# Longformer attention and a cosine-gated MLP on one core: the front's DMA order behind waits for value blocks, six MLP units moved into the front

## The chip, the core and the metric

The kernel runs on one of the eight cores of a Trainium2 chip. The metric is device time in microseconds (us) of one execution. The profile is of one execution, taken by the hardware profiler; its times are counted from the start of its span. Five engines work beside each other, each through its own list in order: TensorE (PE, matmuls; PEld is its weight load), VectorE (DVE), ScalarE (ACT), GpSimd (POOL), and SyncE (SP), which here only issues DMAs. POOL issues DMAs too, all those that change the type of the data on the way. DMAs of both run on the same 16 DMA engines.

## What is computed

The reference, cut to its core: attention over 8 batches of 8 heads with 576 positions of 64, in which a position sees its neighbours up to 32 away and 8 global positions, which also see all; then an MLP on the 4,608 rows of 512.

```python
mask = np.abs(pos[:, None] - pos[None, :]) <= 32
mask = mask | is_global[:, None] | is_global[None, :]
scores = np.where(mask, scale * np.matmul(q, k.transpose(0, 1, 3, 2)), -1e9)
attn = softmax(scores)                     # by rows
x = np.matmul(attn, v).transpose(0, 2, 1, 3).reshape(4608, 512)
h = x @ w_in                               # 512 x 2048
out = (h * np.cos(h)) @ w_out              # 2048 x 512
```

## The kernel before

**Units of work.** Attention goes by pairs of heads (32 pairs, four to a batch), two pairs to a step s (s=0 to 15). Inputs come in half batches, which are the two pairs of one s. The MLP goes by 9 tiles of 512 rows; one *unit* ("1", `one`, `mlp_in`) is one of 16 column blocks of a tile: four matmuls into ph, the cosine (L500, ScalarE), the product g (L501, VectorE). An *out* ("2", `two`, `mlp_out`) is four matmuls of the second layer; every fourth is followed by a copy of po and a store.

**Order.** It is written out by hand: each engine's list is the order in which the program's lines call it. A string of steps is walked through, FRONT for the first four pairs, THIRD for s=2, ORDER for s=3 on. Letters with a pair's number: k and q (`local_k`, `local_q`: transposes on PE and evictions into kw and qb, L406 to L437), s (`scores`: matmuls, exponential L449, mask L450), p (`values`: matmuls into pv, the one PSUM tile for it, then the division into xn, L463 to L469), x (`turn_x`: transposes into xT; after a batch's fourth pair POOL copies the 8 global columns, L489), g (`globals_kq`: POOL copies global keys and queries into kw and qb), n (`x_squares`, ScalarE).

**DMAs.** POOL issues, in one queue: L (`load_qk`, k and q of a half batch with a cast, L257), c (`cast_half`, v of a half batch to fp16 in DRAM, L246), W (`load_w_in`, a quarter of w_in, L642), O (`load_w_out`, a quarter of w_out, L646), gathers of the global rows (L284), casts of k and q to DRAM (L250, half batch 4 on). SP issues, in one queue: the value blocks of a pair from the cast v into vw (`load_v`, L296 to L304; four buffers), the global values from vgw (`load_vg`, L309), transposing loads of k and q (L262, L263), stores. A pair's value block is 2,688 rows of 128 bytes: (80 + 32) x 2 and 2 x 11 x 112.

**Steps that matter below.** In s=2 "G" (`casts`) makes POOL wait, by copying one element of xn into gate (L672), and then gather k, q and v of the next global rows; "b" (`copy_globals`) makes ScalarE copy the gathered kg and qg (L368), "t" turns them. "I" loads eight indices into POOL's registers (L662). A unit may be called only for a tile whose rows are ready (`ready`). In the front, `turned` takes its PSUM from the tag "h", later from "s".

```python
        STEPS = {"s": scores, "p": values, "x": turn_x}
        ...
        for s in range(2, B * NP // 2):
            outs_by[0] = 4 * (s - 2) if s < 5 else 8 * (s - 3)
```

Of the kernel before, what the change touches and what calls it, by code (L numbers as in the profile page):

```python
# [9 lines left out]
FP32 = mybir.dt.float32  # L10
FP16 = mybir.dt.float16
# [6 lines left out]
B, H, S, D = 8, 8, 576, 64  # L18
NT, DM, DFF = 4608, 512, 2048
P = 128  # L20
# [3 lines left out]
G = 8  # L24
# [14 lines left out]

ORDER = "sa0 sa1 sa2 2 2 2 sz0 2 sz1 sz2 pa 1 1 2 xa pz G 1 1 2 xz n 1 1 2 kc qc 1 b kd qd 2 t 1"  # L40

THIRD = "sa0 sa1 sa2 sz0 sz1 sz2 1 1 pa 1 1 xa pz G 1 1 kc qc xz 1 1 b kd qd 1 n t 1"

FRONT = ("g0 s0.0 s0.1 s0.2 c1 k1 q1 g1 B s1.0 s1.1 s1.2 v2 v3 g2 g3 W0 L2 c2 k2 q2 p0 s2.0 x0 s2.1 s2.2 W1 I "
         "k3 q3 p1 s3.0 x1 s3.1 s3.2 L3 c3 g4 g5 k4 q4 p2 v4 v5 W2 x2 p3 W3 k5 q5 x3 n0 v6 v7 g6 g7 O0 O1 O2 O3")
OK_ALL = float(P * (B * NP * 2 * BP + B))


def view(ap, *dims):

    return bass.AP(ap.tensor, ap.offset, [ap.ap[0], *[list(d) for d in dims]])


def dview(ap, offset, *dims):

    return bass.AP(ap.tensor, ap.offset + offset, [list(d) for d in dims])
# [134 lines left out]
def kernel(  # L191
# [10 lines left out]
    nc = tc.nc  # L202
# [5 lines left out]
    keep = es.enter_context(tc.tile_pool(name="keep", bufs=1))  # L208
    work = es.enter_context(tc.tile_pool(name="work", bufs=2))
    ps = es.enter_context(tc.tile_pool(name="ps", bufs=2, space=PSUM))  # L210
# [4 lines left out]
    zero16 = const.tile([P, 1], FP16)  # L215
# [15 lines left out]
    NV = 4  # L231
# [4 lines left out]
    vw = [keep.tile([P, 2, NB, D + 1], FP16, name=f"vw{i}") for i in range(NV)]  # L236
# [4 lines left out]
    def cast_half(s, which):  # L241

        base = s * 4 * S * D
        for x in which:
            if x == "v":
                nc.gpsimd.dma_start(v16[s * 4 * S : (s + 1) * 4 * S].rearrange("(n r) d -> n (r d)", r=16),  # L246
                                    dview(v, base, (16 * D, 4 * S // 16), (1, 16 * D)))
            else:
                src, dst = {"k": (k, k16), "q": (q, q16)}[x]
                nc.gpsimd.dma_start(dst[s].rearrange("t (h d) -> t h d", h=4),  # L250
                                    dview(src, base, (D, S), (S * D, 4), (1, D)))

    def load_qk(s):

        base = s * 4 * S * D
        for src, dst in ((k, kn[s % 2]), (q, qn[s % 2])):
            nc.gpsimd.dma_start(dst.rearrange("x h r d -> x h (r d)"),  # L257
                                dview(src, base, (RW * D, KG), (S * D, 4), (1, RW * D)))
# [24 lines left out]
    def gather(src, dst, n):  # L283
        nc.gpsimd.indirect_dma_start(  # L284
            out=dst, out_offset=None, in_=src.rearrange("b h s d -> (b h s) d"),
            in_offset=bass.IndirectOffsetOnAxis(ap=gidx_rows[:, 0:1], axis=0),
            element_offset=n * 2 * GP * S * D)
# [4 lines left out]
    def load_v(pr):  # L292


        vt, n0, p0 = vw[pr % NV], 2 * pr * S * D, G + KL
        nc.sync.dma_start(vt[p0:KW, :, 0, 0:D], dview(v16, n0, (D, W - KL), (S * D, 2), (1, D)))  # L296
        nc.sync.dma_start(vt[G:p0, :, 0, 0:D], dview(v16, n0 + (S - KL) * D, (D, KL), (S * D, 2), (1, D)))
        for h in range(2):
            lo, i1 = n0 + (h * S - KL) * D, NB
            if pr % 2 and h:  # L300

                i1 = NB - 1
                nc.sync.dma_start(vt[G : KW - KL, h, i1, 0:D], dview(v16, lo + QB * i1 * D, (D, W - KL), (1, D)))
            nc.sync.dma_start(vt[G:KW, h, 1:i1, 0:D], dview(v16, lo + QB * D, (D, W), (QB * D, i1 - 1), (1, D)))  # L304

    def load_vg(pr):
        for h in range(2):
            p0 = (pr % GP * 2 + h) * G
            nc.sync.dma_start(vw[pr % NV][0:G, h], vgw[p0 : p0 + G])  # L309
# [55 lines left out]
    def copy_globals(which):  # L365
        for x in which:
            g16 = g16_of[x] = work.tile([P, 2, D], FP16, tag="g16", name="g16")
            nc.scalar.copy(g16, view({"k": kg32, "q": qg32}[x], (0, 2), (1, D)))  # L368
# [9 lines left out]
    def spread_globals():  # L378
        nc.scalar.copy(vgw[:, :, 0:D], view(vg32, (0, NB), (1, D)))
# [10 lines left out]
    pm_of, xn_of, xg_of, g_of, po_of = ({} for _ in range(5))  # L390
# [9 lines left out]
    def turned(src, pr):  # L400

        t = ps.tile([P, RW, KG], FP16, tag="h" if front[0] else "s", bufs=2 if front[0] else 3)
        h0 = 2 * (pr % 2)
        for r in range(RW):
            for h in range(2):
                nc.tensor.transpose(t[h * D : (h + 1) * D, r], src[:, h0 + h, r], ident16[:KG, :KG])  # L406
        return t
# [18 lines left out]
    def local_q(pr):  # L426
        if pr < 2 * HY:
            t = turned(qn[pr // 2 % 2], pr)
        for h in range(2):
            hp = slice(h * D, (h + 1) * D)  # L430
            to = qb[pr % NK][hp, :, h, G:]
            if pr < 2 * HY:
                copy = nc.scalar.copy if h == 0 else nc.vector.tensor_copy
                copy(view(to, (2 * C, NB), (RW, QB // RW), (1, RW)),
                     view(t[hp], (QB // RW, NB), (1, QB // RW), (KG, RW)))
            else:
                nc.vector.tensor_copy(to, view(qT[pr // 2 % 2][hp, pr % 2], (QB, NB), (1, QB)))  # L437
# [53 lines left out]
    def mlp_in(t, f):  # L491
        if f == 0:
            g_of[t] = work.tile([P, NF, TT], FP16, tag="g", name="g")
        g16 = g_of[t]
        ph = ps.tile([P, TT], FP32, tag="h", bufs=2)
        for j in range(NC):
            nc.tensor.matmul(ph, w_in16[:, j, f * P : (f + 1) * P], xT[:, j, t * TT : (t + 1) * TT],  # L497
                             start=(j == 0), stop=(j == NC - 1))
        cos = work.tile([P, TT], FP16, tag="cos", bufs=3)
        nc.scalar.activation(cos, ph, AF.Sin, bias=pio2)  # L500
        nc.vector.tensor_tensor(g16[:, f], cos, ph, ALU.mult)  # L501
# [77 lines left out]
    def one(n=1):  # L579
        for _ in range(n):  # L580

            if ins_q and ins_q[0][0] < ready[0] and ins_q[0][0] < outs_q[0][0] + 2:
                t, f = ins_q.pop(0)
                mlp_in(t, f)
                ready[1] = t * NF + f + 1
# [10 lines left out]
    ready = [0, 0]  # L596
    tail, front = [False], [True]
# [3 lines left out]
    with tc.manual_schedule():  # L601
# [22 lines left out]
        gather(k, kg32, 0)  # L624
        gather(q, qg32, 0)
        cast_half(0, "v")
        gather(v, vg32, 0)
        load_qk(1)
        copy_globals("k")
        local_k(0)  # L630
        copy_globals("q")
        turn_globals("kq", 0)
        build_mask()
        local_q(0)
        load_v(0)
        load_v(1)
        pv = ps.tile([P, 2, 512], FP32, tag="pv", bufs=1)
        nc.vector.memset(pv, 0.0)
        nc.vector.memset(view(pv[:, :, D : D + 1], (512, 2), (65, 6)), 1.0)

        def load_w_in(c):
            nc.gpsimd.dma_start(w_in16[:, :, c * 512 : (c + 1) * 512],  # L642
# [7 lines left out]
            load_v(pr)  # L650
            load_vg(pr)

        def first_globals(_):
            spread_globals()
            load_vg(0)
            load_vg(1)

        pool_idx = []

# [6 lines left out]
        def globals_kq(pr):  # L666
            globals_k(pr)
            globals_q(pr)

        def casts(s):  # L670

            nc.gpsimd.tensor_copy(gate, xn_of[s][0:1, 1, 0, 0:1])  # L672
            if s % 4 == 2 and s // 4 < 3:
                for src, dst in ((k, kg32), (q, qg32), (v, vg32)):
                    gather(src, dst, s // 4 + 1)
            for n in range(4, 2 * B):
                if s == (n - 2 if n < 7 else n - 3):
                    cast_half(n, "vkq")

        gate = keep.tile([1, 1], FP16)  # L680
        LOCAL = {"k": local_k, "q": local_q}
        OTHER = LOCAL | {"g": globals_kq, "L": load_qk, "W": load_w_in, "c": lambda s: cast_half(s, "v"), "v": load_values, "n": x_squares,
                 "I": load_idx, "O": load_w_out, "B": first_globals}
        for step in FRONT.split():
            f = (STEPS | OTHER)[step[0]]
            f(*[int(x) for x in (step[1:] or "0").split(".")])
        ready[0], front[0] = 1, False
        for i in range(2):
            nc.vector.memset(kT[i][:, :, KL + S :], 0.0)
        make_identity(nc, ident)  # L690
# [1 line left out]
        for s in range(2, B * NP // 2):  # L692
            outs_by[0] = 4 * (s - 2) if s < 5 else 8 * (s - 3)
            for pr in (2 * s + 2, 2 * s + 3):
                if 8 <= pr < B * NP:
                    globals_kq(pr)
            for step in (THIRD if s == 2 else ORDER).split():
                if step == "1":
# [15 lines left out]
                else:  # L714
                    f, pr = (STEPS | LOCAL)[step[0]], 2 * s + "azcd".index(step[1])
# [57 lines left out]
```

## Time and profile before

| what | us |
|---|---|
| three runs | 396.55 (median), 399.38, 394.51 |
| the profiled execution | 397.23 |
| its span | 395.5 |
| busy in the span: PE, DVE, ACT, POOL | 330.8, 254.7, 247.0, 120.1 |
| PE busy in 0 to 60, 60 to 100, 100 to 120, 120 to 140 | 24.1, 30.9, 15.5, 20.0 |

The engines' busy time, by stretches of 10 us; the columns are the stretch, its length, busy us (and instructions) of PE, PEld, DVE, ACT, POOL, the granted clock of PE, the DMA engines' share, and GB/s moved:

```profile
30.00:40.00 10.00, 3.27 (x50) 3.02 (x50) 4.65 (x11) 4.25 (x8) 5.63 (x13) 1.00 1.38 192
40.00:50.00 10.00, 1.91 (x30) 1.57 (x31) 2.04 (x6) 0.00 (x0) 0.00 (x0) 1.00 1.32 173
50.00:60.00 10.00, 6.94 (x90) 5.58 (x90) 5.38 (x16) 7.23 (x12) 4.20 (x16) 1.00 0.65 84
70.00:80.00 10.00, 4.67 (x46) 2.21 (x44) 3.84 (x7) 5.37 (x10) 6.13 (x7) 0.82 1.69 196
120.00:130.00 10.00, 10.00 (x107) 5.68 (x106) 8.97 (x23) 5.78 (x10) 1.86 (x7) 1.00 1.79 144
```

A row of a timeline gives start, duration, engine, line, operation, output and inputs, and in brackets how long the engine had been idle before it and what ended that. A row of a chain of waits gives start, duration and what was on the chain. A row of the waits gives who waited for whom, the us in all, how often, and the longest.

### The profile page before, as it was taken

The page shows a single profiled execution, that of the slowest core. Times are in us where ns is not written, and L with a number is a line of the kernel's source. Part 1 is how long each engine was busy: PE and PEld are TensorE (multiplying, and loading weights), DVE is VectorE, ACT ScalarE, POOL GpSimd, SP SyncE. Part 2 cuts the span into 40 slices and gives each one's busy share as a digit, 9 for nine tenths or more (in the row PEclk, how much of TensorE's full clock was granted, in tenths as well). Part 3 has the DMA queues.
Part 4 walks back from the last instruction along what each step waited for, and adds up shares of the span by engine and source line. Part 5 has one row for each costly group of instructions (what it writes and reads, how often), then busy time and mean ns, then how long its engine had stood idle before and what let it go on. Part 6 is the DMA issues. An engine that isn't in the chain of part 4 may idle for free.

```text
span 395.5 us, 7721 instructions
## 1 busy us (share of the span) xinstructions
PE 330.8 (84%) x2778; PEld 178.2 (45%) x2778; DVE 254.7 (64%) x605; ACT 247.0 (62%) x379; POOL 120.1 (30%) x261
## 2 busy tenths in 40 slices
PE   0373169479779997899999999999999879999993
PEld 0363154244435553455555455555555334444441
DVE  4554257357688787878888897888879344544300
ACT  6754074596575875777767877776787866244300
POOL 7255034614272717073251717323000100000000
PEclk9999999869999999999999999999999999999999
DMA  5999969986999999999999899997820000010121
GB/s 79 149 162 190 176 85 140 203 118 81 153 141 147 157 174 169 126 169 153 192 128 196 144 131 149 182 187 106 168 72 29 27 0 28 37 44 27 53 81 60
DMA packets 186767, 47.60 MB, mean 120 GB/s; under 512 B 174754, under 2 KB 181666, under 8 KB 186466
## 3 DMA queue, kind: packets, MB, share of 16 engines
q0 software_dynamic: 64000, 18.75, 48.1%
q1 hardware_dynamic: 122722, 28.28, 45.1%
q8 instruction: 24, 0.39, 0.4%
q14 instruction: 21, 0.17, 0.1%
HBM read 48.05 MB, written 21.23 MB: 175 GB/s over the span
## 4 chain that ended last, share of the span: by engine, by line
PE 67%; ACT 11%; issue 8%; DMA 5%; DVE 5%; POOL 1%; SPq 1%; ACTq 0%; POOLq 0%; DVEq 0%
PE po L511 28%; PE ph L497 28%; PE st L447 4%; DMA kg<-in_k_dram,gidx_rows 4%; PE pv L458 3%; ACT cos L500 3%; PE tx L481 2%; DVE g L501 2%; ACT kw L414 2%; ACT e L449 1%; ACT sq L530 1%; DVE xn L469 1%; ACT L449 1%; DMA vw<-vgw 1%; DMA gidx_col<-in_global_idx_dram 1%
## 5 line engine op out<-in xcount | busy, mean ns | idle before, releaser
L497 PE MATMUL ph<-xT,w_in 128*128 128x512 f16 x576 | 144.3, 388 | 6.9 <-DVE g L501 5.0
L500 ACT ACTIVATE cos<-ph,pio 128x512 f16<-128x512 f32 x144 | 97.2, 686 | 71.3 <-PE ph L497 67.2
L511 PE MATMUL po<-w_out,g 128*128 128x512 f16 x576 | 140.6, 380 | 1.0 <-DVE o L518 0.9
L501 DVE TENSOR_TENSOR g<-cos,ph 128x512 f16<-128x512 f16 x144 | 96.9, 685 | 59.6 <-ACT cos L500 57.6
L497 PEld LDWEIGHTS <-w_in 128*128 128x128 f16 x576 | 54.1, 99 | 70.0 <-issue 14.5
L511 PEld LDWEIGHTS <-g 128*128 128x128 f16 x576 | 55.5, 98 | 64.1 <-issue 1.9
L449 ACT ACTIVATE e<-st 120x448 f16<-120x448 f32 x96 | 46.3, 544 | 20.7 <-PE st L447 18.3
L450 DVE TENSOR_TENSOR pm<-e,mask 120x448 f16<-120x448 f16 x96 | 37.4, 393 | 21.8 <-ACT e L449 18.8
L447 PE MATMUL st<-qb,kw 128*120 128x112 f16 x384 | 33.1, 236 | 15.1 <-ACT e L449 4.8
L672 POOL COPY gate<-xn 1x1 f16<-1x1 f16 x14 | 2.5, 179 | 137.0 <-DVE xn L469 137.0
L447 PEld LDWEIGHTS <-kw 128*120 128x120 f16 x384 | 31.9, 152 | 24.6 <-issue 12.3
L469 DVE TENSOR_TENSOR xn<-pv,r_all 128x768 f16<-128x768 f32 x32 | 30.6, 957 | 1.9
L458 PE MATMUL pv<-vw,pm 120*56 120x65 f16 x768 | 20.2, 203 | 11.6 <-DMA vw<-v 10.7
L250 POOL DMA_DIRECT2D q<-in_q_dram x12 | 27.4, 2281 | 0.0
L489 POOL COPY xT<-xg 128x4 f16 x64 | 22.1, 345 | 8.4 <-DVE xT L484 4.8
L516 ACT COPY o<-po 128x512 f32<-128x512 f32 x18 | 10.5, 585 | 22.2 <-PE po L511 22.0
L530 ACT ACTIVATE sq<-xn 128x1536 f16<-128x1536 f16 x16 | 23.6, 1474 | 0.0
L458 PEld LDWEIGHTS <-pm 120*56 120x56 f16 x768 | 16.3, 113 | 15.3 <-issue 11.2
L481 PE MATMUL tx<-ident,xn 128*128 128x128 f16 x192 | 17.3, 231 | 5.9 <-DVE xn L469 5.2
L250 POOL DMA_DIRECT2D k<-in_k_dram x12 | 21.1, 1759 | 0.0
L518 DVE COPY o<-po 128x512 f32<-128x512 f32 x18 | 12.3, 685 | 12.1 <-PE po L511 12.0
L481 PEld LDWEIGHTS <-xn 128*128 128x128 f16 x192 | 13.6, 103 | 13.9 <-DVE xn L469 8.4
(106 smaller groups left out, 277.6 us busy)
## 6 DMA issues: line engine op xcount, KB each, us to landing
out_dram<-o SPq DMA_DIRECT2D x36, 256.0 KB
vw<-v SPq DMA_DIRECT2D x48, 154.0 KB
v<-in_v_dram POOLq DMA_DIRECT2D x16, 288.0 KB, 5.1
k<-in_k_dram POOLq DMA_DIRECT2D x12, 288.0 KB, 7.1
q<-in_q_dram POOLq DMA_DIRECT2D x12, 288.0 KB, 10.3
vw<-v SPq DMA_DIRECT2D x16, 140.0 KB
w_in<-in_moe_w_in_dram POOLq DMA_DIRECT2D x4, 512.0 KB
w_out<-in_moe_w_out_dram POOLq DMA_DIRECT2D x4, 512.0 KB, 14.1
```

Source lines behind the costliest of these rows:

```text
L250: nc.gpsimd.dma_start(dst[s].rearrange("t (h d) -> t h d", h=4), dview(src, base, (D, S), (S * D, 4), (1, D)))
L447: nc.tensor.matmul(st[:, j], kp[:, 4 * g + j], view(qp[:, 4 * g + j], (1, 2 * C)), start=True, stop=True)
L449: nc.scalar.activation(e, st, AF.Exp, scale=scale)
L450: nc.vector.tensor_tensor(view(pm[:, 4 * g], (1, n)), view(e, (1, n)), view(mask[:, 4 * g], (1, n)), ALU.mult)
L458: nc.tensor.matmul(pv[r0 : r0 + C, j // 6, c0 : c0 + 65], pm[:, j, h], vp[0:KW, h, j], start=True, stop=True)
L469: nc.vector.tensor_tensor(view(xn, (384, 2), (D, 6), (1, D)), view(pv, (512, 2), (65, 6), (1, D)), view(rp, (6, 2), (1, 6), (0, D)), ALU.mult)
L481: nc.tensor.transpose(tx[:, n], xn[:, n], ident16)
L497: nc.tensor.matmul(ph, w_in16[:, j, f * P : (f + 1) * P], xT[:, j, t * TT : (t + 1) * TT], start=(j == 0), stop=(j == NC - 1))
L500: nc.scalar.activation(cos, ph, AF.Sin, bias=pio2)
L501: nc.vector.tensor_tensor(g16[:, f], cos, ph, ALU.mult)
L511: nc.tensor.matmul(po, g16[:, f, s * P : (s + 1) * P], w_out16[:, f], start=(f == 0), stop=(f == NF - 1))
L530: nc.scalar.activation(sq, view(xn, (1, 2 * BP * P)), AF.Square, accum_out=x_sq[:, s : s + 1])
```

## The change

The order of the front is written anew. FRONT and THIRD, and what stands ahead of them:

```diff
-THIRD = "sa0 sa1 sa2 sz0 sz1 sz2 1 1 pa 1 1 xa pz G 1 1 kc qc xz 1 1 b kd qd 1 n t 1"
-
-FRONT = ("g0 s0.0 s0.1 s0.2 c1 k1 q1 g1 B s1.0 s1.1 s1.2 v2 v3 g2 g3 W0 L2 c2 k2 q2 p0 s2.0 x0 s2.1 s2.2 W1 I "
-         "k3 q3 p1 s3.0 x1 s3.1 s3.2 L3 c3 g4 g5 k4 q4 p2 v4 v5 W2 x2 p3 W3 k5 q5 x3 n0 v6 v7 g6 g7 O0 O1 O2 O3")
+THIRD = "sa0 sa1 sa2 sz0 sz1 sz2 1 pa 1 xa pz G 1 1 kc qc xz 1 1 b kd qd 1 n t 1"
+
+FRONT = ("g0 k1 q1 s0.0 s0.1 s0.2 g1 s1.0 s1.1 s1.2 g2 g3 k2 q2 p0 s2.0 s2.1 s2.2 k3 q3 p1 x0 s3.0 s3.1 s3.2 I w3 W0 L2 W1 c2 c3 "
+         "p2 x1 p3 x2 x3 g4 g5 v4 v5 1 1 k4 q4 w5 W2 L3 W3 1 1 k5 q5 n0 1 1 v6 v7 g6 g7 w7 O0 O1 O2 O3")
...
-                copy = nc.scalar.copy if h == 0 else nc.vector.tensor_copy
+                copy = nc.scalar.copy if h == 0 and pr > 1 else nc.vector.tensor_copy
...
         cast_half(0, "v")
+        cast_half(1, "v")
         gather(v, vg32, 0)
         load_qk(1)
+        pv = ps.tile([P, 2, 512], FP32, tag="pv", bufs=1)
+        nc.scalar.copy(view(pv, (1, 1024)), view(zero16, (0, 1024)))
...
         load_v(0)
-        load_v(1)
-        pv = ps.tile([P, 2, 512], FP32, tag="pv", bufs=1)
-        nc.vector.memset(pv, 0.0)
-        nc.vector.memset(view(pv[:, :, D : D + 1], (512, 2), (65, 6)), 1.0)
+        spread_globals()
+        load_vg(0)
+        for pr in (1, 2, 3):
+            load_v(pr)
+            load_vg(pr)
...
+        def wait_values(pr):
+
+            nc.gpsimd.tensor_copy(gate[32:33], vw[pr % NV][32:33, 1, 5, 0:1])
+
+        def units(_):
+            ready[0], front[0] = 1, False
+            one()
```

- "w" with a pair's number (`wait_values`) is a *gate*: POOL copies one element of that pair's value block and so waits until its last `load_v` DMA has landed (not for `load_vg`). There are three: w3 ahead of W0, L2, W1, c2, c3; w5 ahead of W2, L3, W3; w7 ahead of O0 to O3.
- The cast of v for pairs 2 and 3 ("c1") is issued right behind the first, ahead of the gather of global values. All value blocks of pairs 0 to 3 are issued on SP in one go, ahead of FRONT.
- In the front's part of the order pair 1's k and q come ahead of pair 0's scores; x0 behind p1; p2 to x3 directly after the scores; k4, q4, k5, q5 after these.
- Six units stand in the front ("1", `units`) and two fewer in THIRD, so 14 in place of 10 have run by the end of s=2. With 16 to the tile, and the second tile ready only at the end of s=3, two are left for s=3, where there were six.
- Both halves of pair 0's and pair 1's queries are evicted by VectorE; pv is cleared by ScalarE.

From s=3 on the strings are the same.

More of the change, by code (lines that the diff above doesn't have):

```diff
@@ L634 @@
         local_q(0)
+        nc.vector.memset(view(pv[:, :, D : D + 1], (512, 2), (65, 6)), 1.0)
         load_v(0)
-        load_v(1)
-        pv = ps.tile([P, 2, 512], FP32, tag="pv", bufs=1)
-        nc.vector.memset(pv, 0.0)
-        nc.vector.memset(view(pv[:, :, D : D + 1], (512, 2), (65, 6)), 1.0)
+        spread_globals()
[3 more added lines that the diff above has]
+            load_vg(pr)
         def load_w_in(c):
@@ L651, in load_values @@
             load_vg(pr)
[L653 to L656, printed above, removed]
+        def wait_values(pr):
[3 more added lines that the diff above has]
+            one()
         pool_idx = []
@@ L670, in casts @@
         def casts(s):
-            nc.gpsimd.tensor_copy(gate, xn_of[s][0:1, 1, 0, 0:1])
+            nc.gpsimd.tensor_copy(gate[0:1], xn_of[s][0:1, 1, 0, 0:1])
             if s % 4 == 2 and s // 4 < 3:
@@ L678, in casts @@
                     cast_half(n, "vkq")
-        gate = keep.tile([1, 1], FP16)
+        gate = keep.tile([P, 1], FP16)
         LOCAL = {"k": local_k, "q": local_q}
         OTHER = LOCAL | {"g": globals_kq, "L": load_qk, "W": load_w_in, "c": lambda s: cast_half(s, "v"), "v": load_values, "n": x_squares,
-                 "I": load_idx, "O": load_w_out, "B": first_globals}
+                 "I": load_idx, "O": load_w_out, "w": wait_values, "1": units}
         for step in FRONT.split():
@@ L686 @@
             f(*[int(x) for x in (step[1:] or "0").split(".")])
-        ready[0], front[0] = 1, False
         for i in range(2):
```

## The prediction

> **What bounds the kernel now.** I read the page's 40 slices (9.9 us each) first: PE is mostly at 9 from slice 12 on (about 120 us), and well below in all of them before, least in slice 4 (about 40 to 49 us). Then the chain that ended last, in order of time:
>
> ```profile
> PE   0373169479779997899999999999999879999993
> ```
>
> ```profile
> 4.40 6.30 DMA kg<-in_k_dram,gidx_rows
> ...
> 37.63 1.55 POOL w_in L642 x2
> 39.17 14.28 issue
> ...
> 58.52 3.59 PE ph L497 x8
> ...
> 68.52 7.87 DMA kg<-in_k_dram,gidx_rows
> 76.90 1.00 ACT kw L414
> ```
>
> Two things here cost time and move with the change: a hole of 14 us, and the second gather of global keys, which step s=2 copies at its "b". From 120 us on PE is busy 20.00 of every 20 us, so what is won or lost before about 100 us stays to the end. The waits up to 90 us and the timelines say what the two are:
>
> ```profile
> PE pv L458 <- DMA vw<-v: 10.7, 2, 6.6
> ACT g L368 <- DMA kg<-in_k_dram,gidx_rows: 6.4, 2, 3.6
> ```
>
> ```profile
> 21.33 0.80 POOL L642 DMA_DIRECT2D w_in<-in_moe_w_in_dram  x1
> 22.12 0.75 POOL L257 DMA_DIRECT2D kn<-in_k_dram  x1
> ...
> 59.95 2.96 POOL L646 DMA_DIRECT2D w_out<-in_moe_w_out_dram  x4
> ...
> 68.52 1.04 POOL L284 DMA_INDIRECT kg<-in_k_dram,gidx_rows  x1 [0.16 <-issue]
> ```
>
> ```profile
> 23.29 0.44 SPq L296 DMA_DIRECT2D vw<-v  x1
> ...
> 29.34 5.92 SPq L309 DMA_DIRECT2D vw<-vgw  x2
> 35.30 0.47 SPq L296 DMA_DIRECT2D vw<-v  x1
> ...
> 55.74 0.37 SPq L296 DMA_DIRECT2D vw<-v  x1
> ...
> 57.82 1.47 SPq L309 DMA_DIRECT2D vw<-vgw  x2
> ```
>
> The value blocks of pair 2 take SP from 23.29 to 35.26 (12.0 us) beside POOL's copies of weights and half batches; those of pair 6, with no copy beside them, from 55.74 to 59.29 (3.6). That is the hole: p2 starts at 42.56 and p3 at 50.35. The gather of global keys is issued at 68.52 and lands at 76.38 because four w_out copies of 512 KB stand ahead of it on POOL's queue; ACT has waited since 73.57. I call its landing T. All that s=2 still has to do after T, up to the first exponential of s=3 at 84.50 (8.1 us), is tied to it.
>
> **The change, part by part.**
>
> *Small edits.* The clearing of pv goes from VectorE (0.91 us at 15.17) to ScalarE: 1,024 elements, by L614's 1,344 in 1.23 us about 1.0 us, in ScalarE's wait for kg (7.16 to 10.72); uncovered it would be that 1.0. Queries of pairs 0 and 1: two VectorE copies of 0.76 replace 0.63 on ScalarE and then 0.76 on VectorE (VectorE waited for ScalarE), so 0.1 us on the path. The second cast of v (288 KB) goes ahead of the gather of vg and of kn, qn of pairs 2 and 3: at 180 GB/s (window 8 to 12 us, copies only) 1.6 us later for these. vg is wanted at 13.35, comes at about 14.0; kn, qn are wanted at 18.9. Bounds 0 to 1.5; I take 0.7.
>
> *Front up to the weights.* k1 and q1 stand ahead of the scores of pair 0, x0 no longer stands in the middle of scores. Step by step with the rows' durations: q0 transposed 13.49, its copies 15.0, q1's 16 transposes 15.7, scores of pair 0 at 15.75, exponentials 16.4 to 17.85; q1's copies and POOL's global columns of pair 1 end at 17.4, scores 17.45, exponentials to 19.5; k2 evicted (1.09 + 0.29) 21.0, q2 to 22.4; scores 22.45, exponentials 24.5; k3 evicted 26.0 (30.33 before). The value rows of pairs 0 to 3 now run without weights beside them: SP at 3.6 to 3.9 us a pair (pair 6; pair 11, 109.24 to 113.13) from about 16.3 puts pair 3 at about 29.4. p2 then runs at 28.9, p3 at 32.3, x3 is copied by 36.8, POOL's eight columns (3.06) end at 40.0. So the hole is gone: ph starts at 40.0, 18.5 earlier.
>
> *What then holds.* Six units stand between that and s=2. ScalarE alone, from the first cosine's end: six cosines at 0.69, k4, k5 evicted with q's first half (2.1 each), x_sq 1.7, two table loads at 1.28, PE's cold start (8 matmuls 3.57): the first exponential of s=2 comes at about 54.7, against 55.32 now. So the hole is filled with units, not cut out; the six are missing later, two in s=2 ahead of "b" and four in s=3.
>
> *The gates.* Queued behind a gate is all that POOL has left. First gate: it stands behind the eight index loads (24.2 to 29.55, 5.35 us), which start after k3's copy at 26.2, so POOL gets to it at 31.6 and the values (29.4) are there: no wait, but w_in's first copy goes at 31.7 instead of 21.33. Ahead of and with the cast for pairs 4 and 5 stand 512 + 576 + 512 + 288 = 1,888 KB. At 180 to 205 GB/s (8:12 and 44:48) plus 2 to 3 us of start and landing that is 12.2 to 13.5; by the row of w_out (2,048 KB, 59.95 to 76.38, with rows beside) 15.1. I take 14: 45.7. Pairs 4 and 5 on SP 7.5, less the last 1.3 (vgw, not waited for) plus a landing of 1.6 (p0 is released at 23.37 by the second of four issues from 20.39 to 23.18, which ended at about 21.8): 53.5. Second gate opens, W2, L3 and W3 (1,600 KB) go: at the row of w_out 12.8, to 66.4. Pairs 6 and 7 start at 53.3 and run beside them, where pair 2 took 12.0 us and pair 3 7.8; so they are not done before the copies are, and the rest of about half a pair takes 1.6: third gate at 68. w_out goes at 68.2 (59.95 before) and the gather behind it: 16.4 us by its row, or 2,048 KB at 190 GB/s and 3 us, 13.8, with SP's rows now gone; 14.3: **T = 82.5**, 6.1 later. k7's eviction, casts, transposes and vw loads of s=2 hang on T or on POOL's queue behind it, as now.
>
> *After T.* Same steps to s=3's first exponential. In s=3 two units are left of six: VectorE loses four g of 0.69, 2.8 us, ahead of the copies of k8, q8 that end that step; and PE's wait for VectorE's o copy at 101.0 (0.9) goes, with some 0.3 around it, since all four outs are done in s=3: 4.0 less. Bounds 2.3 (if POOL's columns, to 100.28, end that step) and 4.5.
>
> Sum: 397.23 + 0.0 (small edits and the front, hidden ahead of T) + 6.1 - 4.0 = 399.3 in the profile's terms; that execution lies 0.68 above the median of the three, so **398.6**. T's bounds with each other's: 78 to 87 in this case, so 394 to 405.
>
> A rule on the same row: the Trainium skill, "DMA: Bandwidth & Descriptors", section "Queues, rings and completion order", says that each DMA engine takes turns between the queues it has work for, a packet at a time. The trace bears it out so far that pair 2's rows of 128 bytes take 12.0 us beside copies whose packets are 1 KB, and pair 6's 3.6 alone. By that rule a pair has 2,688 rows against some 190 packets of copies in a us, an estimate of 14 us a pair; it would speak for the third rival below.
>
> **The rivals.**
>
> *Copies get through undisturbed (faster).* If pairs 4 to 7 need no more than 3.5 us a pair and the copies run at 205 GB/s, the cast for pairs 4, 5 lands at 43.9, W2 goes at 50.8, the third gate opens before W3 has landed, and 3,648 KB run in one stretch: 2 + 17.8 + 1.1, T = 71.7. 397.23 - 4.7 - 4.5 - 0.68 = 387.4. For it: 205 and 216 GB/s in some windows of now, and pair 3's 7.8 us. Against it: pairs 2 and 7 beside copies (SP held at 62.48 for 6.26 us).
>
> *The gates add up (slower).* One mechanism: at the third gate POOL, and w_out and the gather behind it, wait for value rows that crawl beside W2, L3 and W3. If these copies land at 67.4 (15.1 and 12.9 by w_out's row), a whole pair (3.6) is then left, and w_out needs its 16.4: T = 87.6; 397.23 + 11.2 - 2.3 - 0.68 = 405.4. It decides the sign from T above 80.4 on, and 2% from T of about 88.
>
> *The hole was all there was.* If "b" did not wait for T (it is reached at about 71, by two units less than 73.57), s=2 would end 2 to 3 us sooner than now and the whole would be near 390. It needs T at 71, so it falls in with the first rival.
>
> *The first gate does nothing* is already in the sum: the index loads keep POOL longer than the values do.
>
> **How the numbers follow.** 2% is 7.9 us, about what a measurement of this kernel can tell from no change (its three runs span 1.2%). Chance of my case, T between 78 and 87: 0.5, at 398.6. First rival with the third: 0.18 at about 387 (nearly all of it over 2%, with what I have not seen in the front). Slower rival: 0.32, at 405 and above, since the terms of the chain of gates are in series and an error in any of them adds. Range: 389 to 408. Faster 0.18, same 0.48, slower 0.34 (my case reaches 405).
>
> **What would show it.** In the changed profile: p2 and p3 without a wait of over 2 us and no hole at 40 to 50; first ph at about 40 and the first exponential of s=2 at about 55; the first w_in issue at about 31.7 right behind the index loads; POOL's gate copies for pairs 5 and 7 with long waits, ended by DMA, at about 53.5 and 68; w_out's issue at about 68; ACT's L368 wait for kg of about 10 us, ended at about 82.5; s=3 some 4 us shorter than now. I am wrong if w_out is issued before 62 or kg lands before 76, if "b" is reached after T, or if PE is not again full from s=5 on.

## The result, and the profile after

The changed kernel takes 409.91 us (median of four executions, 408.57 to 413.64) against 396.98 of the kernel before on the same chip (394.51 to 399.38): a ratio of 1.034, 95% interval 1.025 to 1.044. The profiled execution took 410.63, its span 408.9 (before: 397.23 and 395.5), so the two traces differ by 13.4 us, about as the medians do.

The profile's 40 slices of the changed kernel (10.2 us each):

```profile
PE   0573909219497999699999999999999979999993
```

Counted from 0, slice 4, the hole of before, is full; but slices 5, 7 and 8 are nearly empty, and slice 16 (164 to 174 us, step s=6) shows a new dent of 6. The stretches of 10 us say the same in busy time, with the columns as before:

```profile
30.00:40.00 10.00, 4.18 (x63) 3.28 (x63) 5.26 (x17) 1.19 (x1) 5.33 (x13) 1.00 0.73 103
40.00:50.00 10.00, 8.71 (x88) 4.15 (x88) 3.46 (x6) 6.25 (x11) 2.05 (x10) 1.00 0.91 162
50.00:60.00 10.00, 1.15 (x14) 0.85 (x12) 3.40 (x9) 5.24 (x8) 2.81 (x5) 0.78 0.84 104
70.00:80.00 10.00, 4.53 (x82) 2.51 (x74) 3.66 (x7) 3.55 (x6) 4.99 (x10) 0.80 0.58 76
80.00:90.00 10.00, 0.29 (x1) 0.20 (x2) 0.00 (x0) 0.98 (x3) 5.90 (x6) 0.50 1.22 201
```

PE does 8.71 us in 40 to 50 (1.91 before). From 80 to 90 it does 0.29: the kernel then waits for one transfer, and the last column shows the DMA engines busy at 201 GB/s, most of it with w_out, which stands ahead of it. In 30 to 40, behind the first gate, they move 103 GB/s where they moved 192. The waits up to 98 us of the changed kernel name the transfer:

```profile
POOL gate L660 <- DMA vw<-v: 28.7, 3, 11.7
ACT g L368 <- DMA kg<-in_k_dram,gidx_rows: 18.1, 2, 15.4
PE st L447 <- POOL kw L419: 9.6, 1, 9.6
```

ScalarE's longest wait at L368 is the one for the second gather, 15.4 us; before, that wait was 2.8. Its rows in the timelines, of before and of the changed kernel:

```profile
76.41 0.30 ACT L368 CAST g<-kg 128x128 f16<-128x128 f32 x1 [2.84 <-DMA kg<-in_k_dram,gidx_rows]
```

```profile
89.02 0.30 ACT L368 CAST g<-kg 128x128 f16<-128x128 f32 x1 [15.38 <-DMA kg<-in_k_dram,gidx_rows]
```

The third row of the waits is new: the key copy of pair 5 (L419, POOL) stands behind the second gate, and PE's scores of that pair wait for it. The timeline of the changed kernel shows how the gates pass, and what waits behind them:

```profile
33.67 0.18 POOL L660 COPY gate<-vw 1x1 f16<-1x1 f16 x1 [6.89 <-DMA vw<-v]
34.17 0.79 POOL L647 DMA_DIRECT2D w_in<-in_moe_w_in_dram  x1 [0.32 <-issue]
...
47.45 0.31 SPq L296 DMA_DIRECT2D vw<-v  x1
...
56.88 0.18 POOL L660 COPY gate<-vw 1x1 f16<-1x1 f16 x1 [10.19 <-DMA vw<-v]
57.37 0.80 POOL L647 DMA_DIRECT2D w_in<-in_moe_w_in_dram  x1 [0.30 <-issue]
...
74.14 0.18 POOL L660 COPY gate<-vw 1x1 f16<-1x1 f16 x1 [11.66 <-DMA vw<-v]
74.61 2.98 POOL L651 DMA_DIRECT2D w_out<-in_moe_w_out_dram  x4 [0.29 <-issue]
```

Each cycle is a wait, then copies, then the value rows of two pairs, then the next wait: W0 goes 12.8 us later than before, w_out 14.7 later. The chain that ended last runs straight through it; of the changed kernel's chain:

```profile
53.50 3.26 DMA vw<-v
...
63.69 10.32 DMA vw<-v
74.61 1.32 POOL w_out L651 x2
...
78.50 10.50 DMA kg<-in_k_dram,gidx_rows
```

The last row block of pair 7, issued at 63.69, needs 10.32 us beside W2, L3 and W3. The gather is on the chain once more, and lands at 89.0: T, 12.6 later than before.

### The profile page after: what moved, and what is told of

Same layout as the page of the kernel before. It is cut to its first block, busy times and chain, and to the rows that moved or that the text cites. A ratio compares the mean times of both kernels' runs of the same rounds, so it can differ in the third digit from the quotient of the medians.

```text
span 408.9 us, 7734 instructions
## 1 busy us (share of the span) xinstructions
PE 332.7 (81%) x2778; PEld 178.7 (44%) x2778; DVE 258.2 (63%) x606; ACT 248.7 (61%) x380; POOL 120.1 (29%) x264
## 4 chain that ended last, share of the span: by engine, by line
PE 64%; DMA 11%; ACT 8%; issue 4%; DVE 4%; SPq 3%; POOL 3%; POOLq 0%; ACTq 0%; DVEq 0%
PE po L511 27%; PE ph L497 26%; DMA vw<-v 5%; PE st L447 4%; DMA kg<-in_k_dram,gidx_rows 4%; PE pv L458 3%; PE tx L481 2%; ACT cos L500 2%; DVE g L501 2%; SPq L309 1%; SPq L303 1%; ACT e L449 1%; ACT L449 1%; ACT sq L530 1%; POOL xT L489 1%
## 5 line engine op out<-in xcount | busy, mean ns | idle before, releaser
L511 PE MATMUL po<-w_out,g 128*128 128x512 f16 x576 | 142.6, 385 | 0.0
L501 DVE TENSOR_TENSOR g<-cos,ph 128x512 f16<-128x512 f16 x144 | 96.9, 686 | 62.2 <-ACT cos L500 60.1
L497 PEld LDWEIGHTS <-w_in 128*128 128x128 f16 x576 | 54.1, 99 | 72.2 <-issue 14.4
L449 ACT ACTIVATE e<-st 120x448 f16<-120x448 f32 x96 | 46.3, 545 | 27.4 <-PE st L447 24.6
L447 PEld LDWEIGHTS <-kw 128*120 128x120 f16 x384 | 32.2, 154 | 33.5 <-POOL kw L419 10.5
L516 ACT COPY o<-po 128x512 f32<-128x512 f32 x18 | 10.5, 584 | 22.2 <-PE po L511 22.0
L434 DVE COPY qb<-t 64x576 f16<-64x576 f16 x10 | 7.6, 758 | 24.8 <-ACT qb L434 23.0
L489 POOL COPY xT<-xg 128x4 f16 x64 | 21.1, 329 | 6.9 <-DVE xT L484 3.5
```

The costliest lines, as they stand in the source:

```text
L447: nc.tensor.matmul(st[:, j], kp[:, 4 * g + j], view(qp[:, 4 * g + j], (1, 2 * C)), start=True, stop=True)
L449: nc.scalar.activation(e, st, AF.Exp, scale=scale)
L511: nc.tensor.matmul(po, g16[:, f, s * P : (s + 1) * P], w_out16[:, f], start=(f == 0), stop=(f == NF - 1))
```

## The experiments

Most numbers below are the start of the first exponential (L449) of a step s, as its difference to the profiled execution of before. It shows in which step time is lost. Each is read from one trace, so small differences between runs say little: runs 4 and 18 are the same kernel on two chips, and differ by 3.9 at s=2 and by about 2 at s=3 and s=15. The changed kernel and all eighteen runs, each with the ratio to the kernel before that ran beside it on the same chip (compare ratios; the times are from several chips):

| run | kernel | us | ratio (95%) | s=2 | s=3 | s=4 | s=6 | s=8 | s=15 |
|---|---|---|---|---|---|---|---|---|---|
| | changed | 409.91 | 1.034 (1.025-1.044) | -1.5 | 12.6 | 11.4 | 11.6 | 13.4 | 13.3 |
| 1 | changed, no third gate | 407.42 | 1.021 (1.009-1.033) | -1.1 | 6.8 | 5.6 | 7.0 | 9.4 | 9.9 |
| 2 | changed, no gates | 406.63 | 1.017 (1.003-1.031) | -1.8 | 4.4 | 4.3 | 5.5 | 8.6 | 8.8 |
| 3 | changed, gather first | 407.86 | 1.023 (1.010-1.035) | -2.3 | -2.5 | 0.4 | 1.6 | 9.8 | 9.6 |
| 4 | before, gather first | 398.39 | 0.989 (0.983-0.996) | 1.2 | -3.8 | -3.3 | -3.1 | -3.4 | -3.1 |
| 5 | no gates, copies early | 404.46 | 1.016 (1.012-1.019) | 12.4 | 4.8 | 3.6 | 3.8 | 8.7 | 8.4 |
| 6 | before, first gate | 402.03 | 1.009 (1.003-1.015) | -2.6 | 4.1 | 4.1 | 4.1 | 4.5 | 4.6 |
| 7 | as 5, gather first | 402.96 | 1.012 (1.008-1.017) | 12.2 | 4.5 | 3.2 | 3.9 | 5.6 | 5.8 |
| 8 | changed, units back | 408.16 | 1.027 (1.020-1.034) | -7.0 | 11.0 | 11.9 | 13.5 | 15.1 | 15.5 |
| 9 | as 4, changed prologue | 400.12 | 1.004 (1.000-1.009) | -0.3 | -4.0 | -3.1 | -1.5 | 4.3 | 4.1 |
| 10 | as 9, W0 and W1 late | 400.01 | 1.006 (1.002-1.011) | 1.4 | -1.9 | -2.3 | -2.1 | 2.8 | 2.7 |
| 11 | before, three gates | 411.14 | 1.034 (1.017-1.050) | -2.0 | 10.5 | 10.5 | 10.5 | 13.8 | 14.3 |
| 12 | as 7, units back | 398.58 | 1.002 (0.998-1.006) | 4.3 | -1.9 | -2.6 | -2.5 | -0.7 | -0.8 |
| 13 | changed, even casts | 407.94 | 1.019 (1.009-1.029) | -1.9 | 11.4 | 10.2 | 9.9 | 9.3 | 9.9 |
| 14 | as 3, even casts | 400.88 | 1.001 (0.996-1.006) | -2.2 | -0.6 | 0.8 | 1.0 | 2.1 | 6.7 |
| 15 | as 4, even casts | 395.57 | no interval | -0.9 | -4.5 | -4.2 | -5.5 | -4.3 | -3.4 |
| 16 | before, third gate | 406.33 | 1.013 (1.003-1.023) | 2.0 | 5.8 | 5.2 | 5.2 | 6.7 | 7.8 |
| 17 | 15 repeated | 393.97 | 0.985 (0.979-0.990) | -2.3 | -5.8 | -6.1 | -7.4 | -6.3 | -5.6 |
| 18 | 4 repeated | 398.59 | 0.999 (0.995-1.002) | -2.7 | -6.0 | -6.3 | -6.1 | -1.0 | -1.0 |

### Taking the gates and the gather's place out of the changed kernel (1 to 3)

Run 1 takes out the third gate, run 2 all three:

```diff
-g6 g7 w7 O0
+g6 g7 O0
```

```diff
-I w3 W0
+I W0
...
-q4 w5 W2
+q4 W2
...
-g6 g7 w7 O0
+g6 g7 O0
```

Run 3 keeps all gates and issues s=2's gathers ("H") ahead of the third, so that T no longer stands behind w_out:

```diff
-g6 g7 w7 O0
+g6 g7 H w7 O0
...
-            if s % 4 == 2 and s // 4 < 3:
+            if s % 4 == 2 and 0 < s // 4 < 3:
```

> Changed kernel without the third gate (w7), so POOL issues w_out right behind pair 7's global columns, at about 62.5 instead of 74.6. Theory of the gates in series: w_in's rest and w_out run in one stretch, about 3,700 KB from 59.4 at 160 to 170 KB a us, T (the landing of the second gather of kg) at about 82 instead of 89.0, everything after it 6 to 7 us earlier: 402 to 404 us, ratio to the kernel before about 1.015. Rival 'the DMA engines are full either way': the rows of pair 7 and w_out only trade places, T stays within 2 us of 89, 408 to 410 us. Rival 'pair 5's key copy behind the second gate is what makes s=2 late': nothing changes, since w5 stays, 409 us.

> Changed kernel without all three gates, its order otherwise kept. Gates in series: first w_in copy at about 32.3 instead of 34.2, the last two and L3 at about 47 instead of 57.4, w_out at about 50.5 instead of 74.6, T at about 73; but value rows of pairs 4 and 5 now run beside copies at some 12 us a pair, so p5 comes at about 70. s=3 starts some 13 us earlier than with the gates: about 396 us, ratio about 0.995 to 1.0. Rival 'DMA engines are full either way': T at 87 to 89, 407 to 410 us. Rival 'pair 5's key copy': scores of pair 5 come at about 54 instead of 60.7, but the total moves only by 0 to 2 us if T does not.

> Changed kernel with all gates, but the second gathers of k, q and v stand ahead of the third gate and w_out on POOL's queue (out of step G of s=2). Gates in series with T as what they cost: kg lands at about 72 behind the rest of w_in, step b (reached at 73.6) does not wait, first exponential of s=3 at about 82 instead of 97.1; then the casts of k and q of half batch 4, still behind w_out, become the next late thing (landing about 91 and 93, wanted at 91): 394 to 398 us, ratio 0.99 to 1.005. Rival 'T is not what binds, w_out itself or the values are': s=3 starts by less than 4 us earlier, 405 to 409 us.

Runs 1 and 3 did at s=3 what they should or nearly so. In run 1 kg lands at 83.2 (82 expected) and s=3 starts 5.8 us earlier than in the changed kernel; in run 3 the first exponential is at 82.05. Run 2's s=3 starts 8.3 us earlier, not 13. Of the ratios only run 1's 1.021 has the expected value, 1.015, within its interval, and by its trace only 3.4 of the 5.8 us are left at s=15; runs 2 and 3 miss theirs. Run 2, although it has no gate, still issues W0 at 32.2, behind the index loads, and POOL's wait for xn grows to 20 us, because the values of pairs 4 and 5 now run beside copies. Run 3 lost its gain between s=6 and s=8.

So T behind w_out is what bounds s=3 in the changed kernel. All traces say the same: in the seven in which ScalarE waits for kg at "b" (before, changed, runs 1, 8, 11, 13, 16), the first exponential of s=3 comes 8.1 us after T, with T from 76.4 to 89.0. But T is not alone: two more limits stand close behind it. Where ScalarE does not wait for kg, it can still reach "b" late (at 80.8 in run 2, against 73.6 in the changed kernel), and the step s=6 can take a gain back. Without its gates the changed kernel keeps half of its loss, 1.017.

### Putting the gates alone into the kernel before (6, 16, 11)

Order, units and the values' place stay as before; run 6 adds the first gate (and with it moves W0, L2, c2, W1 behind the index loads), run 16 the third, run 11 all three (the second, "w5", stands ahead of W2 there too):

```diff
-g2 g3 W0 L2 c2 k2
+g2 g3 k2
...
-s2.1 s2.2 W1 I
+s2.1 s2.2 I
...
-s3.1 s3.2 L3
+s3.1 s3.2 w3 W0 L2 c2 W1 L3
```

```diff
-v4 v5 W2
+v4 v5 w5 W2
...
-g6 g7 O0
+g6 g7 w7 O0
```

> The kernel before with the first gate alone: W0, L2, c2, W1 behind the index loads and a wait for pair 3's value block, the rest of its order as it was. Theory 'bytes': about 5,800 KB moved by 50 us, T at 85 to 88, the first exponential of s=4 9 to 11 later than before, time 405 to 409, ratio 1.020 to 1.030, although the hole at 40 to 55 us closes. Theory 'the later gates': the first gate costs nothing, since the values of pairs 2 and 3 come 10 us sooner; then 392 to 398.

> The kernel before with the third gate alone, ahead of w_out. Pair 7's rows, alone, should be there at 63 to 64 (SP issued pair 6's last at 59.3), so w_out goes some 4 us later than 59.95, T is at 80 to 81, s=3 3 to 5 us later: ratio 1.006 to 1.014. If a gate costs only behind another: 0.997 to 1.004.

> The sixth experiment's kernel (before with the first gate) with the second gate ahead of W2 and the third ahead of w_out; units and order of steps as before. If the gates are the change's cost, in series (T near 89 as in the changed kernel): ratio 1.025 to 1.035. If the rest of the change (units, order, values ahead) costs half of it: 1.010 to 1.020.

Run 6 loses 4.1 us by s=4: neither theory's number, for "bytes" had 9 to 11. It closes the hole only in part. PE no longer waits there for values, but 6.6 us for the keys that L2 now brings later, and p2 starts at 44.0, against 42.6 before. Nor is it T that costs the 4.1: w_out goes 2.5 us earlier than before, at 57.4, and ScalarE reaches "b" at 80.5 without a wait for kg. PE had waited 8.1 us for the values of pair 5, whose rows now run beside w_out; from the waits of run 6 from 60 to 120 us:

```profile
PE pv L458 <- DMA vw<-vgw: 9.2, 3, 8.1
```

Run 16's ratio was within its range, and here the wait acts through T: 5.8 us later than before, and s=3 with it. A gate costs by itself. Run 11 is the main finding: the three gates alone, with the copies that they hold back, give 1.034, the whole of the change's loss; T is 10.5 us later, and s=3 too. Its timeline has the same staircase as the changed kernel, with the second and third gates within 3 us of it:

```profile
34.28 0.18 POOL L655 COPY gate<-vw 1x1 f16<-1x1 f16 x1 [3.37 <-DMA vw<-v]
...
59.03 0.18 POOL L655 COPY gate<-vw 1x1 f16<-1x1 f16 x1 [14.22 <-DMA vw<-v]
...
71.19 0.18 POOL L655 COPY gate<-vw 1x1 f16<-1x1 f16 x1 [5.99 <-DMA vw<-v]
71.67 2.97 POOL L646 DMA_DIRECT2D w_out<-in_moe_w_out_dram  x4 [0.29 <-issue]
```

By s=4 the first gate alone costs 4.1, the third alone 5.2 (2.0 of it stand in run 16's trace at s=2 already, ahead of its gate), all three 10.5. Since run 6's loss does not go through T and run 16's does, these are not terms of one sum, and what the second gate adds is not resolved. Beside the gates, the new order, the six units and the early values together change the total by nothing that the comparison resolves; without gates they do cost, as the next runs show.

### Where the copies stand without gates (5, 7, 12, 9, 10)

If gates cost by starting copies late, the copies can be put back to where they were. Run 5 does this in the changed order without gates; run 7 adds the early gathers; run 12 also puts the units back:

```diff
-g2 g3 k2
+g2 g3 W0 L2 c2 k2
...
-s2.2 k3
+s2.2 W1 k3
...
-s3.2 I w3 W0 L2 W1 c2 c3 "
+s3.2 L3 c3 I "
...
-p2 x1
+W2 W3 p2 x1
...
-k4 q4 w5 W2 L3 W3 1 1
+k4 q4 1 1
...
-g6 g7 w7 O0
+g6 g7 O0
```

> The changed kernel without its three gates, and with POOL's first copies where the kernel before had them: W0, L2, c2 behind g3 (about 21 us), W1 behind s2.2, L3, c3 behind s3.2, W2, W3 ahead of p2. Against the second experiment only the place of these copies differs. Theory 'bytes': what is late at T and later is the volume that the DMA engines have moved; the change leaves them about 1.8 MB behind at 50 us (5,758 KB against 7,591) because W0 and all behind it start at 32 to 34 us. Then here about 7,400 KB have moved by 50 us, the first exponential of s=4 comes at or ahead of before's (-3 to +2) and the time is 393 to 399. Theory 'order of the steps': the order of PE's and ScalarE's work and the units in the front cost the time; then 403 to 407 as in the second experiment. Theory 'rows beside copies': the rows of pairs 2 and 3 crawl again beside W0 and L2, the hole is back, and the time is 398 to 402.

> The kernel of the fifth experiment with the second gathers ahead of w_out. Theory 'bytes': the fifth experiment's time less what T still held there, 2 to 6 us: 389 to 395, below the kernel before; w_out's 2 MB are then behind the gather, and s=6 must not wait for values again (under 3 us). Rival: as in the third experiment the gain at s=3 is lost again in s=5 to s=8, and the time is that of the fifth within 1.5 us.

> The seventh experiment's kernel with the six units back in s=2 and s=3. If its late front (first exponential of s=2 at 67.5) is the units standing ahead of k4, q4, k5, q5: s=2 starts at 56 to 60, s=3 at 82 to 84, ratio 0.99 to 1.00. If it is pair 2's values: s=2 starts some 8 us earlier, but s=3 and s=4 give 4 of it back: 1.00 to 1.01.

Run 5 refutes the theory that counts only the volume moved: 7,549 KB had gone by 50 us, as wanted (5,758 in the changed kernel, 7,591 before), and the time was 404.5. That time is what the theory of the order of the steps gave (403 to 407), above the 398 to 402 of rows beside copies; the trace shows that the rows of pair 2 do crawl again, so both have a part. The waits from 20 to 60 us of run 5:

```profile
PE pv L458 <- DMA vw<-vgw: 13.9, 3, 12.9
```

So the first gates did what they say, they kept the rows of pairs 2 to 5 and the copies apart; with the copies back in their old places the crawl is back, and the units then stand in a row behind it: s=2 starts at 67.7. Run 12, without the six early units, is 1% faster than run 7, its s=2 starts 7.8 us earlier and its ratio is that of the kernel before: there the units cost. That they do so because nothing passes them in PE's list is argued. Runs 9 and 10 try the changed prologue alone in the kernel of run 4, and then W0 and W1 behind c3:

```diff
-g2 g3 W0 L2 c2
+g2 g3 L2 c2
...
-s2.2 W1 I
+s2.2 I
...
-L3 c3 g4
+L3 c3 W0 W1 g4
```

> The fourth experiment's kernel (before, second gathers ahead of w_out) with the changed kernel's prologue alone: second cast of v behind the first, value blocks of pairs 0 to 3 issued in one go, queries of two pairs by VectorE. No gate, units where they were, order of steps as before. If what keeps the seventh experiment at 1.012 is its order of steps and its six early units: as the fourth experiment, ratio 0.983 to 0.995. If it is the early values (their rows run into W0, L2 and c2 and hold SP): 1.003 to 1.015, with a wait of PE for vw of 8 us or more ahead of p2 or p3.

> The same with W0 and W1 behind L3 and c3, no gate: between g3 and the end of pair 3's scores POOL issues only L2 and c2 (864 KB in place of 1,888). Theory 'copies of weights beside rows': pair 3's values come by 36, the hole of 14 us shrinks to under 5, s=2's first exponential comes at 45 to 50, T stays out of the way, and the time is 0.97 to 0.99 of before. Theory 'volume': the weights' 1 MB comes back later beside the values of pairs 4 to 7, and s=3 starts no earlier than in the fourth experiment (80.7): 0.99 to 1.01.

Neither is faster than the kernel before, though both start s=3 earlier. They lose 5.8 and 4.9 us from s=5 to s=8, of which below. So run 9's 1.004, in the range said for values that come too early, is no proof of that: PE waited 6.4 us for values where 8 was said, and the loss comes steps later. In run 10 L2 and c2 alone are enough to slow pair 2's rows, and pair 3's, issued from 31.7 to 44.8, run beside W0 to W3: PE waited 10.3 us for them. Moving the weights did not shorten the crawl.

### The units back (8)

```diff
-v4 v5 1 1 k4 q4 w5 W2 L3 W3 1 1 k5 q5 n0 1 1 v6
+v4 v5 k4 q4 w5 W2 L3 W3 k5 q5 n0 v6
...
-sz2 1 pa 1 xa pz G
+sz2 1 1 pa 1 1 xa pz G
```

> The changed kernel with the six units back in s=2 and s=3 (none in the front); all gates as changed. T stays at 88 to 90 (no gate or copy hangs on a unit). The prediction's price of the units: s=3 4.0 us longer, so the time is that of the changed kernel plus 4: 413 to 415. Reading of the changed kernel's trace: s=3 was held there by VectorE's copy L423 and POOL, not by units, so putting them back costs what before's s=3 took more, 1.2: 410 to 412.

The place where the first unit switches the PSUM tags stays. Neither the 413 to 415 of the prediction's price nor the 410 to 412 of the other reading came as the median. The trace (of an execution of 413.07, the longest of its four) is 2.3 us later at the end than the changed kernel's, 0.5 of it by s=4; the medians (408.16 and 409.91) have the other sign, and the intervals overlap. What the units are worth beside the gates is not resolved and is left open.

### What is lost again between s=6 and s=8 (13, 14)

In run 3 ScalarE waits in s=6, where it spreads the next global values (L379) over the old ones, for SP's last copies of the old ones; from run 3's timeline, and, below it, the same wait in run 14's waits from 120 to 190:

```profile
163.20 0.83 ACT L379 CAST vgw<-vg 128x768 f16<-128x768 f32 x1 [6.05 <-DMA vw<-vgw]
```

```profile
ACT vgw L379 <- DMA out_dram<-o: 1.6, 1, 1.6
```

These copies stand on SP's queue behind the value blocks of pairs 12 to 15, and those behind the casts: s=4 issues two half batches in one go. Runs 13 and 14 cast one half batch in each step:

```diff
-                if s == (n - 2 if n < 7 else n - 3):
+                if s == n - 2:
```

> The changed kernel with one half batch cast in each step (half n in s=n-2 throughout; as it is, s=4 casts two, 6 and 7, and each later step one ahead). Theory 'double cast': the 1.8 us that the changed kernel loses once more from s=5 to s=8 (first exponentials 11.61, then 13.36 later than before's) come from value rows that run beside two half batches; then s=8 is at +11 to +12 and the time 1 to 2 us lower, 407 to 409. Rival: the loss stays, or grows since half 7 is now cast a step later and its rows come later: 409 to 412.

> The third experiment's kernel (changed, second gathers ahead of the third gate) with one half batch cast in each step. Theory 'double cast': the 8.2 us that it lost between s=6 and s=8 stay away: 397 to 401, ratio 0.995 to 1.007, ACT's wait at L379 under 2 us in s=6. Rival 'behind in volume': casts and rows are late as a whole, whatever their order: 405 to 409.

How the casts are spread is the cause: from s=6 to s=8 run 14 loses 1.0 us where run 3 lost 8.2, and its ratio is 1.001 against 1.023, the intervals apart. (The edit takes the double cast out of s=4 and casts half batch 7 and all later ones one step later; which of the two counts isn't told apart.) Run 13 gains 0.6 there, where the changed kernel loses 1.8. (The trace of run 14, of an execution longer than its median, loses 4.6 more between s=10 and s=12; why stays open.) So gains in the front were held down by a second limit in s=4 to s=6, which the prediction did not have.

### A version that is faster than both (4, 15, 17, 18)

Run 4 takes the gathers of s=2 out of its "G" and issues them ahead of w_out in the kernel before; run 15 adds the even casts; 17 and 18 repeat both on one chip with more rounds:

```diff
-g6 g7 O0
+g6 g7 H O0
```

> Kernel before with the same edit: second gathers ahead of w_out in the front. T at about 62 instead of 76.4, no wait of 2.8 us at step b and no half clock of PE behind it (76.3 to 83.1): 391 to 394 us, ratio 0.985 to 0.993. Rival 'b would wait for something else anyway' (the casts behind w_out, vgw's readers): under 1 us, ratio 0.998 to 1.0.

> The fourth experiment's kernel (before, second gathers ahead of w_out) with one half batch cast in each step. It lost nothing from s=5 to s=8, so nothing is to be had: 0.985 to 0.994. If half 7 a step later makes s=6 wait for its rows: 0.995 or more.

> The fifteenth experiment's kernel once more, since its four executions (387 to 401) gave no interval: second gathers ahead of w_out and one half batch cast in each step, in the order of before. By its trace (last steps 3.4 us ahead of before's, as the fourth experiment's 3.1): ratio 0.985 to 0.994. If the even casts cost something in s=6: over 0.995.

> The fourth experiment's kernel once more, on the same chip as the seventeenth: 0.985 to 0.994. If the even casts are worth what the fifteenth trace shows between s=5 and s=7 (1 to 2 us ahead), the seventeenth is 0.3 to 0.5% faster than this one; if not, the two are within 0.3%.

Run 15's four executions lay between 387 and 401 us, too far apart for an interval. Repeated, with both edits the ratio is 0.985 (0.979 to 0.990), beside 0.999 (0.995 to 1.002) for the gathers alone on the same chip: there the gain needs the even casts too. The even casts alone were not run. In run 18 the early gathers bring 6.0 us at s=3, and 5.1 of it is lost from s=6 to s=8; with even casts 1.1 is lost there. Run 4, the same kernel as 18, gave 0.989 on another chip, and its trace loses only 0.3 there; why it does not lose more stays open. From the timeline of run 17:

```profile
58.00 1.04 POOL L284 DMA_INDIRECT kg<-in_k_dram,gidx_rows  x1 [0.32 <-POOL qb L398]
...
61.59 3.12 POOL L646 DMA_DIRECT2D w_out<-in_moe_w_out_dram  x4
```

The gathers that "b" needs no longer stand behind w_out, and ScalarE does not wait for kg there.

## Why the prediction was wrong

The forecast was 398.6, at about the same time as before, with a range up to 408. The step that failed is the chain of the three gates, the term T: it was to be 6.1 us later than before and was 12.6. The rival "The gates add up (slower)" was the right one in sign, and even its 405.4 was short. Step by step:

- **The front up to the weights: right.** k3's copies were done at 26.5 (26.0 said), p2 and p3 ran at 29.5 and 33.8 with no long wait, the first ph came at 40.65 (40.0), the first exponential of s=2 at 53.85 (54.7). The hole is gone. Small edits at nothing: consistent with it.
- **"No wait" at the first gate: wrong by 2.1.** Pair 3's rows were said to be there at 29.4, ahead of POOL; the gate passed at 33.67. SP had issued the last of them at 30.5, and they landed 3.2 after that. "The first gate does nothing" fell with it: run 6 gives it 4.1 us by itself, with what it moves behind the index loads, W0, L2, c2 and W1, though through the values of pair 5 and not through T.
- **The second gate at 53.5: 56.88.** c2's values could start at 47.45 (45.7): W0's 2.5 less 0.7 that the copies were faster than the 14 taken. SP then took 6.5 (6.2), and the landing another 3.0, where 1.6 was read from a row of the start.
- **The third gate at 68: 74.14.** 3.9 from W2's later issue. The copies had landed 13.4 after it (12.8 said), at 70.8. Then the gate waited another 3.3 us, not 1.6. This is near the slower rival's "whole pair (3.6)", but by luck: when the last copy packet was through, 426 of pair 7's 2,688 rows were left, all but 38 of them were gone by 71.7, and the gate waited for the landing of those 38. Pair 7's rows did crawl beside the copies, as the rival said.
- **w_out to T: right.** 14.4 (14.3); T = 89.0, 12.6 later than before and not 6.1. This term was mis-sized by 6.5: three waits in series, sized short by 2.1, 1.3 and 2.8 us, all of one sign. The prediction saw that "an error in any of them adds" and still took the middle of each.
- **After T: right**, 8.1 to the first exponential of s=3 (97.12).
- **Units, -4.0: -1.2.** VectorE was to end s=3 sooner by four g; but PE waited 4.8 for POOL's columns (L489), which stand behind the casts. In both traces the first exponential of s=4 comes 5.9 us after POOL's wait for xn ends, behind the casts and the first columns; that wait ends 8.0 us after the first exponential of s=3, where it was 9.2 before, and this is the 1.2. So POOL's list and not VectorE's ended the step, already before. (VectorE was late as well: its copy L423, 0.17 us before, took 2.97.) POOL's bound, 2.3, was named as possible; the true value lay under it.
- **Left out: +1.9** from s=4 on, the double cast of s=4 meeting value rows (runs 13, 14; part of it could be the early casts after it).

12.6 - 1.2 + 1.9 = 13.3, the difference of the spans to 0.1. (All three are read from the same two traces, so this shows where the time went and is no test of the causes.) The sign was decided by T, as the rival said (from 80.4 on), and 2% at about 88, which T passed by 1. "If 'b' did not wait for T" did not arise: ScalarE reached it at 73.6. The fault lay in that step's landings. For the first two gates one row of the start (1.6) stood for what took 3.2 and 3.0 us, although no copy packet ran in those stretches; for the third it was the last few rows behind the copies. Why so few rows land so late stays open.

## What to carry to other kernels

A wait in a DMA queue that keeps two kinds of transfer apart can save the slow one's crawl, but puts the landing of one in series with the start of the other, for everything behind it in the queue: add landings at the upper end of what the trace shows, since their errors don't cancel. Before separating transfers, look for the one that is late on the path and only stands behind the wrong neighbour: moving three small gathers past a 2 MB copy, and spreading a double cast, gave 1.5% where three waits, with the copies that they held back, cost 3.4%. And when a gain in one step is gone some steps later, look there for the next limit before doubting the first finding.

## What was not expected of the hardware

**Rows and copies share by packets, part of the time.** From 64 to 68 us the changed kernel's trace has 678 rows of 128 bytes and 636 copy packets of 1 KB; from 24 to 34 before has 1,508 rows and 1,473 such packets. In these stretches a row takes as much of a turn as a packet eight times its size. It is not so throughout: from 60 to 63 us, with rows of pair 7 issued, the changed kernel's trace has 485 copy packets and 7 rows. By the rule that the prediction cites (the Trainium skill, "DMA: Bandwidth & Descriptors", section "Queues, rings and completion order"), the trace agrees in the stretches with one to one. Pair 7's rows took 15.0 us from first issue (59.0) to last landing (74.0), by that rule's estimate 14, but the last 3.2 us of it had no copies beside them, so the nearness is in part luck. (What the rule speaks for is the slower rival, second in the prediction's list, not the third.)

**VectorE held while POOL issues casts.** From the timeline of the changed kernel's s=3, by engine:

```profile
106.18 2.97 DVE L423 COPY kT<-kT 128x64 f16<-128x64 f16 x1
```

```profile
106.98 2.17 POOL L250 DMA_DIRECT2D q<-in_q_dram  x1
```

The copy ends at 109.15, as does POOL's issue. In before's trace the twelve copies of this line have a median of 0.196 us. The Trainium skill, "DMA: Bandwidth & Descriptors", section "SWDGE vs HWDGE vs iDMA", says that GpSimd writes its DMA rings into the same SBUF state from which VectorE locks it out in two-port modes; the trace has the other direction, VectorE waiting for POOL. The other runs bear the hold out. In runs 1, 2, 3, 5, 7 and 13 this copy also starts within 1 us after POOL begins to issue the cast of k, takes 2.3 to 3.0 us, and ends with the issue of q to 0.02 us. In the kernel before and in runs 6, 8, 11, 12 and 14 it starts behind both issues and takes 0.17 to 0.25; run 8 is the changed kernel with its units moved. Not every operation of VectorE is held: in the changed kernel's trace the copy out of PSUM (L484) and the product (L501) keep their length beside such issues. Which state the two share, no run shows.

**The clock after idle time.** The granted clock was 0.50 from 76 to 96 us of the changed kernel, where PE waited for T up to 89 us; from 90 to 96 it was still 0.50 although PE was busy for 4.5 of the 6 us, and from 96 to 106 it was 0.97. Over the span it was 0.948 (0.985 before).
